# One step more between a tile's mask and its norm in an attention pipeline, with one guard and one reciprocal for two tiles

## The chip, the cores and the metric

The kernel runs on one core of one Trainium2 chip. The metric is the device time of one execution in microseconds (us). The kernel before takes 1290.63 us, the median of three runs that lie between 1290.49 and 1290.71 us.

The engines are named as in the profile: PE is TensorE's matrix multiply and PEld its weight load, DVE is VectorE, ACT is ScalarE, POOL is GpSimd, SP is SyncE. L309 is line 309 of the kernel file.

## The reference

Three stages follow one another. Attention has 2 batches, 8 heads, 576 rows and head dimension 64; its softmax keeps only scores within `tau` of the row's largest. Then a mixture of 8 experts with a gate that is normalised eight times over rows and columns, and a mixture of 4 experts with given probabilities, both on 1152 rows of 512 columns with 1024 hidden columns.

```python
def _attn_ref(q, k, v, tau):
    scores = (1.0 / np.sqrt(q.shape[-1])) * np.matmul(q, k.transpose(0, 1, 3, 2))
    thresh = np.max(scores, axis=-1, keepdims=True) - tau
    scores = np.where(scores >= thresh, scores, -1000000000.0)
    scores = scores - np.max(scores, axis=-1, keepdims=True)
    attn = np.exp(scores)
    attn = attn / (np.sum(attn, axis=-1, keepdims=True) + 1e-09)
    return np.matmul(attn, v).astype(np.float32)

def _moe_ref(x, w_gate, w1, w2):          # x: 1152 x 512
    P = np.exp(x @ w_gate - (x @ w_gate).max())
    for _ in range(8):
        P /= P.sum(1, keepdims=True) + 1e-09
        P /= P.sum(0, keepdims=True) + 1e-09
        P *= N / E
    for e in range(8):
        out += P[:, e:e + 1] * (np.maximum(x @ w1[e], 0.0) @ w2[e])

def _moe2_ref(x, domain_probs, w1, w2):
    p = domain_probs / (domain_probs.sum(-1, keepdims=True) + 1e-09)
    for e in range(4):
        out += p[:, e:e + 1] * (np.maximum(x @ w1[e], 0.0) @ w2[e])
```

The row sum in the denominator, the 1e-9 that is added to it and the division are what the change touches.

## The kernel before

**Units.** Attention is cut into 72 units (tiles) of 128 rows of queries against all 576 keys. The first 16 units (`exact` in the code) are rows 0 to 255 of batch 0; the next 20 the other 320 rows of batch 0, five for each pair of heads; the last 36 are batch 1, nine for each pair. Products that need more than one pass are made from a rounded high part and a low part (`kh` and `kl`, `eth` and `etl`); the 16 exact units transpose and multiply in fp32 instead, without a low part.

**Steps.** `step` (L415 to L462) is called once for each step t and issues, in program order, one piece of work for each of several units; the order on every engine is this order. In step t before:

- PE transposes unit t-2 into `et` and `er` (`turn`, L327 and L329), and later in the step makes the scores of unit t+2 (L275 for the first four units, L282 after), and the product with v for a unit that ended a group (`mix`, L367 for exact units, L374 and L376 for the others).
- DVE masks unit t (L309: score at or above the threshold times the exponential, in place, with the row sum as a second output), takes the row maximum of unit t+1 (`top`, L287), adds 1e-9 to the sum of unit t (`guard`, L313), works out the threshold of unit t+1 where the unit is exact (`line`, L295 to L298), and takes the reciprocal for unit t (L317). Further down the step it makes the low part of unit t-2's transposed tile (`lo`, L349 and L352) and adds or splits outputs (L385, L396, L502).
- POOL scales unit t in place by the reciprocal (`norm`, L319). It also splits keys, values and weights (L85, L109) and prepares queries (L253 to L257).
- ACT casts unit t-2's transposed tile to its high part (`hi`, L334 and L336), takes the exponential of unit t+1 (L303 or L305), and, for units that aren't exact, its threshold (L292).

There are 72 + 5 steps and a start of two.

**Buffers.** Four exponential tiles `ex` go round, six statistics tiles `st`, one transposed tile `et` (so the next `turn` waits for `hi` and `lo` of the unit before), and two score tiles in use at a time.

**Work beside attention.** `plan` (L194) sets the step in which keys, queries and values of a head are prepared. From unit 16 on, two fillers of an expert layer are issued between the scores and the next transposes (`expert_fill`: L493 and L521 on PE, L499 and L525 on ACT, L502 on DVE); the list `todo` (L592) says from which step each may start, `few` (L598) how many pieces a step may take near the batch border. The rest of the expert layers runs when attention has ended.

Of the kernel before, what the change touches and what calls it, by code (L numbers as in the profile page):

```python
# [9 lines left out]
F32 = mybir.dt.float32  # L10
F32R = mybir.dt.float32r
AF = mybir.ActivationFunctionType
ALU = mybir.AluOpType
# [6 lines left out]
P = 128  # L20
# [5 lines left out]
RA1, RA2 = 3, 4  # L26
# [3 lines left out]
def attention_two_moe_kernel(ctx, tc, qP, kP, qT, kT, vp, tau, wg, w1, w1s, w2, w2s, dp, m2w1s, m2w2, m2w2s, out):  # L30
    nc = tc.nc
    V, A, G, T = nc.vector, nc.scalar, nc.gpsimd, nc.tensor
# [9 lines left out]
    acc = [accp.tile([P, DM], F32, name=f"acc{t}") for t in range(4)]  # L42
# [79 lines left out]
    class Attention:  # L122
# [71 lines left out]
        def plan(self):  # L194

            for i, hd in enumerate(self.heads):
                if hd["ws"]:
                    continue
                old = self.heads[i - 2]
                k, q = i - 4, i - 3  # L200
                v = hd["first"] + 3
                if not old["ws"]:
                    k, v = max(hd["first"] - 5, old["end"] - 2), max(v, old["lastmix"] + 3)
                    q = k + 1
                    if hd["n"] == S and hd["h"] % 2 == 0:
                        v = max(hd["first"] + 2, old["lastmix"] + 3)
                for t, w in zip((k, q, v), self.prep(hd)):
                    self.work.setdefault(t, []).append(w)

# [73 lines left out]
                             start=i == 0, stop=i == len(ops) - 1)  # L283

        def top(self, u):
            st = u["st"] = self.pl.tile([P, 8], F32, tag="st", name="st", bufs=6)
            V.tensor_reduce(st[:, 0:1], u["sc"][:, :, :HS], axis=AX.XY, op=ALU.max, negate=not u["q"][0][0]["ws"])  # L287

        def line(self, u):
# [17 lines left out]
        def mask(self, u):  # L307
            st, ex = u["st"], u["ex"]
            V.scalar_tensor_tensor(ex, u["sc"][:, :, :HS], st[:, 2:3], ex, op0=ALU.is_ge, op1=ALU.mult,  # L309
                                   accum_out=st[:, 3:4])  # L310

        def guard(self, u):
            V.tensor_scalar(u["st"][:, 4:5], u["st"][:, 3:4], 1e-9, None, op0=ALU.add)  # L313

        def norm(self, u):
            st = u["st"]
            V.reciprocal(st[:, 5:6], st[:, 4:5])  # L317
            exf = u["exf"] = u["ex"].rearrange("p a b -> p (a b)")
            G.tensor_scalar(exf, exf, st[:, 5:6], 1.0, op0=ALU.mult, op1=ALU.mult)  # L319

        def turn(self, u):
            eg, exf = u["eg"], u["exf"]
# [92 lines left out]
        def step(self, fill, side):  # L415

            us, t = self.units, self.t
            un = lambda i: us[i] if 0 <= i < len(us) else None
            self.load()
            nxt, a, d, x, c, z, y = (un(t + i) for i in (2, 1, 0, -2, -3, -4, -5))  # L420
            if x:
                self.turn(x)
            if d:
                self.mask(d)
            if a:
                self.top(a)
            if d:
                self.guard(d)
            if a and a["q"][0][0]["exact"]:
                self.line(a)  # L430
            if d:
                self.norm(d)
            for part, u in ((2, y), (1, z), (0, c)):
                for g in u["mix"] if u else ():
                    if g["head"]["exact"]:
                        self.mix(g, part)
            if x:
                self.hi(x)
            for u, late in ((z, False), (y, True)):
                for g in u["mix"] if u else ():  # L440
                    if late == g["head"]["exact"]:
                        self.out(g)
            if a:
                self.exp(a)
                if not a["q"][0][0]["exact"]:
                    self.line(a)
            fill(0, bool(c and c["mix"]))
            if x:
                self.lo(x)
            if nxt:  # L450
                self.scores(nxt)
            self.run(self.later)
            for g in c["mix"] if c else ():
                if not g["head"]["exact"]:
                    self.mix(g, 0)
            fill(1, bool(c and c["mix"] or z and z["mix"]))
            self.run(self.late)
            for w in self.work.pop(t, ()):
                w()
            side()  # L460
            self.t += 1
            return self.t < len(us) + 5  # L462


    def start(t):
# [71 lines left out]
    y1 = [early[:, DM * t:DM * (t + 1)] for t in range(4)]  # L537

    def part(t, at, k, n):
        return t[:, at:at + k * n].rearrange("p (k n) -> p k n", k=k)  # L540

    tail0 = [[part(tails, 512 * j, FT, 64) for j in range(2)],
             [part(tails, 1024 + 1024 * j, FT, P) for j in range(2)]]
# [4 lines left out]
    with ExitStack() as att:  # L548
        ap = pool(att, "attn", side="right")
        ps_s = pool(att, "ps_s", 2, space=PSUM)  # L550
        ps_t = pool(att, "ps_t", 1, space=PSUM)
        ps_r = pool(att, "ps_r", 1, space=PSUM)
        banks.pool = ps = pool(att, "ps_m", 2, space=PSUM)
        at = Attention(ap, ps_s, ps_t, ps_r, ps)
        for p in range(H // 2):
            at.add_pair(0, p, 0, 256, True, p == 0)
        nA0 = len(at.units)
        for p in range(H // 2):
            at.add_pair(0, p, 256, 320, False)
        nA1 = len(at.units)  # L560
        for p in range(H // 2):
            at.add_pair(1, p, 0, S, False)
        at.plan()
        room = [2 * FT]
        at.load()
        drop = on[:, 0:1]
        V.tensor_scalar(drop, tau_sb, 0.0, None, op0=ALU.is_ge)
        V.tensor_scalar(esc, drop, 0.125, None, op0=ALU.mult)
        V.tensor_scalar(lin[:, 0:1], drop, -0.125, None, op0=ALU.mult)
        V.tensor_scalar(drop, drop, -BIG, BIG, op0=ALU.mult, op1=ALU.add)  # L570
        V.scalar_tensor_tensor(lin[:, 1:2], tau_sb, 8.0, drop, op0=ALU.mult, op1=ALU.add)
        V.tensor_tensor(drop, tau_sb, drop, op=ALU.add)
        V.tensor_scalar(on[:, 1:2], drop, -1.0, None, op0=ALU.mult)

        def side():
            if at.t >= -1:
                fetch(2)
            if at.t >= nA0 - 3 and raws and room[0] and (at.t % 3 < 2 if at.t < nA1 else room[0] > 2 or at.t % 2):
                room[0] -= 1
                cook()  # L580
            if at.t == 20:
                nc.sync.dma_start(wg_sb, wg)
                nc.sync.dma_start(dp_sb, dp)
            if at.t == 24:
                split(V, V, wg2[:, :, :E1], wg2[:, :, E1:], wg_sb)

        def free(n):
            room[0] += n

        X0, X1 = Expert(0), Expert(1)  # L590
        near, far = ((0, 0), (1, P)), ((2, 32), (3, 32 + P))
        todo = [(nA0 + 4, expert_fill(hp, X0, 0, 256, near, acc, None, 0, at.later, keep)),  # L592
                (nA1 + 3, expert_fill(hp, X0, 256, 320, far, acc, tail0[0], 0, at.later, free)),
                (nA1 + 3, expert_fill(hp, X1, 0, 256, near, y1, None, 0, at.later, keep)),
                (nA1 + 3, expert_fill(hp, X1, 256, 320, far, y1, tail0[1], 0, at.later, keep))]

        left, spent = [0], [0]
        few = dict(zip(range(nA1 - 3, nA1 + 4), (2, 2, 2, 2, 2, 1, 1)))  # L598

        def pull(n, end=True):  # L600

            for i in range(n):
                if not todo or at.t <= todo[0][0] or (left[0] == 1 and not end):
                    return i
                left[0] = next(todo[0][1], -1)
                if left[0] < 0:
                    todo.pop(0)
                if left[0] <= 0:
                    left[0] = 0
                    return i + 1  # L610
            return n

        def fill(phase, busy):
            if phase == 0:
                if 0 <= at.t < nA0 - 3 and at.t % 2 == 0:
                    room[0] -= 1
                    cook()
                spent[0] = pull(few.get(at.t, 3))
            elif left[0] or not busy:
                pull(max(few.get(at.t, RA1 if at.t < nA1 + 3 else RA2) - spent[0], 0), True)  # L620

        while at.step(fill, side):
            pass
        at.flush()
        while left[0]:
            pull(1)
        at.flush()
        while raws:
            cook()
            fetch(2)  # L630
# [25 lines left out]
    class Psum:  # L656
# [17 lines left out]
        def pair(self):  # L674
            whole = [(self.free.index(k), k ^ 1) for k in self.free if k ^ 1 in self.free[:self.free.index(k)]]
            if not whole:
                return None
            k = self.free[min(whole)[0]] & ~1
            return self.take(k, k + 1)
# [861 lines left out]
```

## Time and profile before

| | us |
|---|---|
| median of three runs | 1290.63 |
| the profiled execution's own time | 1290.54 |
| its span in the trace | 1288.8 |
| attention (first scores to the last product with v) | about 6 to 243 |
| PE busy in the whole span | 1268.6 |
| DVE busy in the whole span | 877.0 |

The profiled execution's own time stands 1.74 us above its span and 0.09 us under the median of the runs. Attention fills about the first fifth of the span; what comes behind it is the rest of the expert layers. Busy times that the trace gives for PE are of a pipelined engine, so a stretch can be called fully busy while matmuls still start late; the list of waits says what ended the idle times.

### The profile page before, as it was taken

What the parts mean: (1) busy time and instruction counts of PE and PEld (TensorE: products, weight loads), DVE (VectorE), ACT (ScalarE), POOL (GpSimd) and SP (SyncE); (2) the same over time, 40 slices, a digit from 0 to 9 for tenths busy, and PEclk for the clock granted to TensorE, in tenths of its full rate; (3) what the DMA queues carried; (4) which work ended last, traced back from release to release, by engine and by line L of the source; (5) the groups of instructions that cost most, each with busy time, mean ns of one, the idle gap of its engine ahead of it and who ended that gap; (6) DMA issues with size and microseconds to landing.
All of it is one profiled execution on the core that took longest, in us unless ns stands there. A gap on an engine that the chain in (4) does not pass through costs nothing.

```text
span 1288.8 us, 25100 instructions
## 1 busy us (share of the span) xinstructions
PE 1268.6 (98%) x9373; PEld 1207.6 (94%) x9373; DVE 877.0 (68%) x1842; ACT 739.1 (57%) x1492; POOL 896.9 (70%) x987
## 2 busy tenths in 40 slices
PE   8998999999999999999999999999999999999998
PEld 5597988888889999999999999999989999999998
DVE  6798888567537666766666666676745667666667
ACT  7887877422546646555554655566546465555552
POOL 7997987405796776867777786777668568677760
PEclk9999999999999999999999999999999999999999
DMA  5542330101221111212111211111212012111102
GB/s 171 160 128 75 97 97 17 41 1 34 66 83 50 42 42 50 58 35 58 50 42 42 52 59 37 52 50 42 58 34 59 25 50 58 35 57 50 42 18 74
DMA packets 43225, 73.84 MB, mean 57 GB/s; under 512 B 5216, under 2 KB 12512, under 8 KB 43104
## 3 DMA queue, kind: packets, MB, share of 16 engines
q1 hardware_dynamic: 42816, 71.96, 19.3%
q8 instruction: 74, 1.21, 0.4%
q14 instruction: 47, 0.39, 0.1%
q10 hardware_dynamic: 288, 0.28, 0.1%
HBM read 69.86 MB, written 2.36 MB: 56 GB/s over the span
## 4 chain that ended last, share of the span: by engine, by line
PE 89%; DVE 4%; POOL 2%; ACT 2%; issue 1%; DMA 1%; SPq 0%; DVEq 0%; POOLq 0%; ACTq 0%
PE mm L1079 36%; PE mm L1391 33%; PE mm L493 5%; PE mm L521 5%; PE mm L1199 3%; PE sc L282 2%; PE et L327 2%; PE pv L367 1%; DVE ex L309 1%; PE pv L376 1%; PE pv L374 1%; DVE st L287 1%; DVE etl L349 1%; ACT ex L305 0%; POOL wl L85 0%
## 5 line engine op out<-in xcount | busy, mean ns | idle before, releaser
L85 POOL TENSOR_TENSOR wl<-raw,wh 128x512 fp32r<-128x512 f32 x217 | 282.3, 1307 | 181.1 <-ACT wh L80 180.9
L1179 DVE SCALAR_TENSOR_TENSOR acc<-mm,p,acc 128x256 f32<-128x256 f32 (+1 forms) x428 | 195.3, 508 | 72.2 <-PE mm L1391 59.3
L1391 PE MATMUL mm<-wh,h 128*128 128x256 f32 x960 | 173.6, 279 | 0.0
L1086 ACT COPY snap<-mm 128x576 f32<-128x576 f32 x126 | 80.9, 642 | 152.5 <-DVE mm L1240 77.9
L80 ACT CAST wh<-raw 128x512 fp32r<-128x512 f32 x217 | 133.5, 627 | 47.2 <-PE mm L1391 26.4
L1391 PEld LDWEIGHTS mm<-wh,h 128*128 128x128 f32 x960 | 146.6, 188 | 0.0
L1079 PE MATMUL mm<-xh,wl 128*128 128x288 f32 x672 | 145.6, 297 | 0.3
L1079 PE MATMUL mm<-xh,wh 128*128 128x288 f32 x672 | 143.4, 294 | 0.0
L1079 PE MATMUL mm<-xl,wh 128*128 128x288 f32 x672 | 143.0, 294 | 0.0
L1391 PE MATMUL mm<-wl,h 128*128 128x256 f32 x480 | 134.6, 280 | 0.0
L1391 PE MATMUL mm<-wh,tails 128*128 128x256 f32 x696 | 126.4, 279 | 0.0
L85 POOL TENSOR_TENSOR wl<-sum,wh 128x512 fp32r<-128x512 f32 x82 | 107.4, 1310 | 8.1 <-ACT wh L80 8.1
L1079 PEld LDWEIGHTS mm<-xh,wl 128*128 128x128 f32 x672 | 106.3, 188 | 3.3 <-DVE mm L1099 0.5
L1079 PE MATMUL mm<-xth,wl 128*128 128x288 f32 x504 | 108.2, 295 | 0.2
L1079 PE MATMUL mm<-xtl,wh 128*128 128x288 f32 x504 | 107.8, 294 | 0.0
L1079 PE MATMUL mm<-xth,wh 128*128 128x288 f32 x504 | 107.5, 294 | 0.0
L1079 PEld LDWEIGHTS mm<-xl,wh 128*128 128x128 f32 x672 | 107.4, 188 | 0.0
L1079 PEld LDWEIGHTS mm<-xh,wh 128*128 128x128 f32 x672 | 107.2, 188 | 0.0
L1391 PEld LDWEIGHTS mm<-wh,tails 128*128 128x128 f32 x696 | 106.2, 188 | 0.0
L80 ACT CAST wh<-sum 128x512 fp32r<-128x512 f32 x82 | 51.5, 628 | 85.4 <-POOL sum L783 72.0
L1391 PE MATMUL mm<-wl,tails 128*128 128x256 f32 x348 | 97.3, 279 | 0.0
L1391 PEld LDWEIGHTS mm<-wl,h 128*128 128x128 f32 x480 | 90.0, 188 | 0.4
(241 smaller groups left out, 3486.2 us busy)
## 6 DMA issues: line engine op xcount, KB each, us to landing
raw<-in_w1s SPq DMA_DIRECT2D x56, 256.0 KB, 2.7
raw<-in_w2s SPq DMA_DIRECT2D x48, 256.0 KB, 2.6
raw<-in_w SPq DMA_DIRECT2D x40, 256.0 KB, 3.1
raw<-in_m2w1s SPq DMA_DIRECT2D x32, 256.0 KB, 2.6
raw<-in_m2w2s SPq DMA_DIRECT2D x28, 256.0 KB, 2.6
kr<-in_kT SPq DMA_DIRECT2D x22, 288.0 KB, 3.1
vr<-in_vp SPq DMA_DIRECT2D x24, 160.0 KB, 2.6
qr<-in_qT SPq DMA_DIRECT2D x8, 288.0 KB, 2.9
```

Of the source, the lines that this page charges most:

```text
L80: A.copy(hi, src)
L85: el.tensor_tensor(lo, src, f(hi), op=ALU.subtract)
L282: T.matmul(sc[:m, hf, :HS], lhsT=q, rhs=kk[:, hf * HS:(hf + 1) * HS], start=i == 0, stop=i == len(ops) - 1)
L287: V.tensor_reduce(st[:, 0:1], u["sc"][:, :, :HS], axis=AX.XY, op=ALU.max, negate=not u["q"][0][0]["ws"])
L327: T.transpose(et[:, kt], exf[:, kt * P:(kt + 1) * P], ident)
L493: T.matmul(ph[:, :n], lhsT=a[:, kt * P:(kt + 1) * P], rhs=x[:, kt, n0:n0 + n], start=i == 0 and kt == 0, stop=i == 2 and kt == KT - 1)
L521: T.matmul(py, lhsT=x, rhs=a, start=i == 0, stop=i == 3 * FT - 1)
L1079: T.matmul(ch[b][:, g, :HS], lhsT=w[:, (2 * g + kt) * P:(2 * g + kt + 1) * P], rhs=operand(u, kt, lo), start=first and j == 0, stop=j == l ...
L1086: A.copy(v[u], m)
L1179: V.scalar_tensor_tensor(a, src, s, a, op0=ALU.mult, op1=ALU.add)
L1199: T.matmul(py, lhsT=hid[x][:, kk, o:o + P], rhs=w[y], start=n == 0, stop=n == 3 * HF - 1)
L1391: T.matmul(m, lhsT=hid(x, kt + ko), rhs=wk[y], start=first and n == 0, stop=n == 5, skip_group_check=True)
```

## The change

The step loop gets one stage more. `mask` puts the row sum of unit t into a tile `two` of eight columns that two units share (an even and the odd unit behind it): columns 0 and 1 hold the two sums, 2 and 3 the sums with 1e-9, 4 and 5 the reciprocals. `guard` runs in odd steps alone, behind `top`, and makes both additions and both reciprocals with two instructions of 128x2. `norm` on POOL scales unit t-1 instead of unit t. `turn` is unit t-3 instead of t-2, the products with v and the outputs come one step later too, and the steps end at 72 + 6. The plan for values, the starts in `todo` and the numbers in `few` are one step later; the preparation of keys and queries stays where it was. `st` has three buffers instead of six, `two` has three.

```diff
--- before.py
+++ after.py
@@ -198,12 +198,12 @@
                     continue
                 old = self.heads[i - 2]
                 k, q = i - 4, i - 3
-                v = hd["first"] + 3
+                v = hd["first"] + 4
                 if not old["ws"]:
-                    k, v = max(hd["first"] - 5, old["end"] - 2), max(v, old["lastmix"] + 3)
+                    k, v = max(hd["first"] - 5, old["end"] - 2), max(v, old["lastmix"] + 4)
                     q = k + 1
                     if hd["n"] == S and hd["h"] % 2 == 0:
-                        v = max(hd["first"] + 2, old["lastmix"] + 3)
+                        v = max(hd["first"] + 3, old["lastmix"] + 4)
                 for t, w in zip((k, q, v), self.prep(hd)):
                     self.work.setdefault(t, []).append(w)
 
@@ -283,7 +283,7 @@
                              start=i == 0, stop=i == len(ops) - 1)
 
         def top(self, u):
-            st = u["st"] = self.pl.tile([P, 8], F32, tag="st", name="st", bufs=6)
+            st = u["st"] = self.pl.tile([P, 8], F32, tag="st", name="st", bufs=3)
             V.tensor_reduce(st[:, 0:1], u["sc"][:, :, :HS], axis=AX.XY, op=ALU.max, negate=not u["q"][0][0]["ws"])
 
         def line(self, u):
@@ -307,16 +307,21 @@
         def mask(self, u):
             st, ex = u["st"], u["ex"]
             V.scalar_tensor_tensor(ex, u["sc"][:, :, :HS], st[:, 2:3], ex, op0=ALU.is_ge, op1=ALU.mult,
-                                   accum_out=st[:, 3:4])
-
-        def guard(self, u):
-            V.tensor_scalar(u["st"][:, 4:5], u["st"][:, 3:4], 1e-9, None, op0=ALU.add)
+                                   accum_out=u["sum"])
+
+        def pair(self, i):
+            if i % 2 == 0:
+                self.two = self.pl.tile([P, 8], F32, tag="two", name="two", bufs=3)
+            u = self.units[i]
+            u["sum"], u["over"] = (self.two[:, k + i % 2:k + i % 2 + 1] for k in (0, 4))
+
+        def guard(self):
+            V.tensor_scalar(self.two[:, 2:4], self.two[:, 0:2], 1e-9, None, op0=ALU.add)
+            V.reciprocal(self.two[:, 4:6], self.two[:, 2:4])
 
         def norm(self, u):
-            st = u["st"]
-            V.reciprocal(st[:, 5:6], st[:, 4:5])
             exf = u["exf"] = u["ex"].rearrange("p a b -> p (a b)")
-            G.tensor_scalar(exf, exf, st[:, 5:6], 1.0, op0=ALU.mult, op1=ALU.mult)
+            G.tensor_scalar(exf, exf, u["over"], 1.0, op0=ALU.mult, op1=ALU.mult)
 
         def turn(self, u):
             eg, exf = u["eg"], u["exf"]
@@ -417,19 +422,20 @@
             us, t = self.units, self.t
             un = lambda i: us[i] if 0 <= i < len(us) else None
             self.load()
-            nxt, a, d, x, c, z, y = (un(t + i) for i in (2, 1, 0, -2, -3, -4, -5))
+            nxt, a, d, e, x, c, z, y = (un(t + i) for i in (2, 1, 0, -1, -3, -4, -5, -6))
             if x:
                 self.turn(x)
             if d:
+                self.pair(t)
                 self.mask(d)
             if a:
                 self.top(a)
-            if d:
-                self.guard(d)
+            if d and t % 2:
+                self.guard()
             if a and a["q"][0][0]["exact"]:
                 self.line(a)
-            if d:
-                self.norm(d)
+            if e:
+                self.norm(e)
             for part, u in ((2, y), (1, z), (0, c)):
                 for g in u["mix"] if u else ():
                     if g["head"]["exact"]:
@@ -459,7 +465,7 @@
                 w()
             side()
             self.t += 1
-            return self.t < len(us) + 5
+            return self.t < len(us) + 6
 
 
     def start(t):
@@ -589,13 +595,13 @@
 
         X0, X1 = Expert(0), Expert(1)
         near, far = ((0, 0), (1, P)), ((2, 32), (3, 32 + P))
-        todo = [(nA0 + 4, expert_fill(hp, X0, 0, 256, near, acc, None, 0, at.later, keep)),
-                (nA1 + 3, expert_fill(hp, X0, 256, 320, far, acc, tail0[0], 0, at.later, free)),
-                (nA1 + 3, expert_fill(hp, X1, 0, 256, near, y1, None, 0, at.later, keep)),
-                (nA1 + 3, expert_fill(hp, X1, 256, 320, far, y1, tail0[1], 0, at.later, keep))]
+        todo = [(nA0 + 5, expert_fill(hp, X0, 0, 256, near, acc, None, 0, at.later, keep)),
+                (nA1 + 4, expert_fill(hp, X0, 256, 320, far, acc, tail0[0], 0, at.later, free)),
+                (nA1 + 4, expert_fill(hp, X1, 0, 256, near, y1, None, 0, at.later, keep)),
+                (nA1 + 4, expert_fill(hp, X1, 256, 320, far, y1, tail0[1], 0, at.later, keep))]
 
         left, spent = [0], [0]
-        few = dict(zip(range(nA1 - 3, nA1 + 4), (2, 2, 2, 2, 2, 1, 1)))
+        few = dict(zip(range(nA1 - 2, nA1 + 5), (2, 2, 2, 2, 2, 1, 1)))
 
         def pull(n, end=True):
 
@@ -617,7 +623,7 @@
                     cook()
                 spent[0] = pull(few.get(at.t, 3))
             elif left[0] or not busy:
-                pull(max(few.get(at.t, RA1 if at.t < nA1 + 3 else RA2) - spent[0], 0), True)
+                pull(max(few.get(at.t, RA1 if at.t < nA1 + 4 else RA2) - spent[0], 0), True)
 
         while at.step(fill, side):
             pass
```

On DVE, among the exact units (`xl` is the low part of an output): what a step holds before the change.

```order
L309 SCALAR_TENSOR_TENSOR ex,st<-sc,st,ex 128x576
L287 TENSOR_REDUCE st<-sc 128x1
L313 TENSOR_SCALAR st<-st 128x1
L295 TENSOR_SCALAR st<-st,on 128x1
L317 RECIPROCAL st<-st 128x1
L385 TENSOR_TENSOR xl<-pv,xh 64x256
```

An even and an odd step of the same units on DVE after:

```order
L309 SCALAR_TENSOR_TENSOR ex,two<-sc,st,ex 128x576
L287 TENSOR_REDUCE st<-sc 128x1
L295 TENSOR_SCALAR st<-st,on 128x1
L309 SCALAR_TENSOR_TENSOR ex,two<-sc,st,ex 128x576
L287 TENSOR_REDUCE st<-sc 128x1
L319 TENSOR_SCALAR two<-two 128x2
L320 RECIPROCAL two<-two 128x2
L295 TENSOR_SCALAR st<-st,on 128x1
L390 TENSOR_TENSOR xl<-pv,xh 64x256
```

An even step has lost both small instructions; an odd step has them side by side, ahead of the threshold (L295) instead of around it.

On DVE, a step later in attention, where a low part `etl` is made in each step (L349 before, L354 after; `hl` is the low part of an expert's hidden tile). Before:

```order
L309 SCALAR_TENSOR_TENSOR ex,st<-sc,st,ex 128x576
L287 TENSOR_REDUCE st<-sc 128x1
L313 TENSOR_SCALAR st<-st 128x1
L317 RECIPROCAL st<-st 128x1
L349 TENSOR_TENSOR etl<-et,eth 128x4x128
L502 SCALAR_TENSOR_TENSOR hl<-mm,hh 128x256
```

After, from an even step's low part over an odd step to the next even one:

```order
L354 TENSOR_TENSOR etl<-et,eth 128x4x128
L357 TENSOR_TENSOR eth<-er,eth 64x384
L508 SCALAR_TENSOR_TENSOR hl<-mm,hh 128x256
L309 SCALAR_TENSOR_TENSOR ex,two<-sc,st,ex 128x576
L287 TENSOR_REDUCE st<-sc 128x1
L319 TENSOR_SCALAR two<-two 128x2
L320 RECIPROCAL two<-two 128x2
L354 TENSOR_TENSOR etl<-et,eth 128x4x128
L508 SCALAR_TENSOR_TENSOR hl<-mm,hh 128x256
L309 SCALAR_TENSOR_TENSOR ex,two<-sc,st,ex 128x576
L287 TENSOR_REDUCE st<-sc 128x1
L354 TENSOR_TENSOR etl<-et,eth 128x4x128
```

In odd steps the low part still stands behind both small instructions, in even steps it follows the maximum directly. In all DVE has 36 guards and 36 reciprocals instead of 72 and 72.

On PE, the start of the program, with the tiles' numbers (`sc` are score tiles, `ex` the unit that is transposed). Before:

```order
L275 MATMUL sc_222<-y1_97 128x288 x2
L327 MATMUL et_225<-ident_68,ex_163 128x128 x4
L329 MATMUL er_226<-ident_68,ex_163 64x128
L282 MATMUL sc_247<-kh_155,qs_168 128x288 x2
L282 MATMUL sc_247<-kl_156,qs_168 128x288 x2
L327 MATMUL et_254<-ident_68,ex_192 128x128 x4
L329 MATMUL er_226<-ident_68,ex_192 64x128
```

After:

```order
L275 MATMUL sc_220<-y1_97 128x288 x2
L282 MATMUL sc_236<-kh_155,qs_168 128x288 x2
L282 MATMUL sc_236<-kl_156,qs_168 128x288 x2
L332 MATMUL et_243<-ident_68,ex_163 128x128 x4
L334 MATMUL er_244<-ident_68,ex_163 64x128
L282 MATMUL sc_260<-kh_155,qs_168 128x288 x2
L282 MATMUL sc_260<-kl_156,qs_168 128x288 x2
```

The scores of the fifth unit now stand ahead of the first transposes, and so on down the program: every transposition and product with v stands one unit's scores later. PE's number of instructions is the same.

## Rows read from the trace of the kernel before

**Rows 1.** The page: busy us of the span, and the chain by engine.

```profile
PE 1268.6 (98%) x9373; PEld 1207.6 (94%) x9373; DVE 877.0 (68%) x1842; ACT 739.1 (57%) x1492; POOL 896.9 (70%) x987
...
PE 89%; DVE 4%; POOL 2%; ACT 2%; issue 1%; DMA 1%; SPq 0%; DVEq 0%; POOLq 0%; ACTq 0%
```

**Rows 2.** Busy us of each engine in stretches of 50 us, with instruction counts.

```profile
0.00:50.00 50.00, 44.04 (x199) 27.30 (x200) 33.88 (x117) 39.80 (x77) 39.09 (x48) 1.00 0.57 167
50.00:100.00 50.00, 47.84 (x324) 39.94 (x325) 43.62 (x113) 41.45 (x94) 46.49 (x57) 1.00 0.45 131
100.00:150.00 50.00, 47.17 (x322) 43.72 (x321) 44.72 (x114) 40.07 (x88) 39.85 (x63) 1.00 0.28 79
...
250.00:300.00 50.00, 50.00 (x311) 43.54 (x310) 33.49 (x94) 13.70 (x35) 15.09 (x14) 1.00 0.04 12
```

**Rows 3.** PE waits from 20 to 250 us: total us, times, longest.

```profile
PE et L327 <- DVE etl L349: 3.9, 7, 1.6
PE sc L282 <- DVE ex L309: 2.2, 4, 1.0
...
PE mm L493 <- DVE xf L396: 0.7, 1, 0.7
```

**Rows 4.** Timeline of DVE: start, us, instruction, idle before and releaser.

```profile
179.92 0.69 DVE L349 TENSOR_TENSOR etl<-et,eth 128x512 fp32r<-128x512 f32 x1 [1.80 <-ACT eth L334]
```

**Rows 5.** Chain of waits at the start: start us, us, what.

```profile
13.95 1.06 PE et L327 x4
...
15.03 0.59 ACT e L334
15.62 0.74 ACT ex L303
...
23.07 0.63 PE et L327 x4
23.70 0.11 PE er L329
23.80 1.72 PE pv L367 x6
25.53 0.73 PE sc L282 x4
...
26.80 1.01 PE pv L367 x4
...
29.09 1.72 PE pv L367 x6
```

**Rows 6.** All L313: ns min, median, max; who waited for it.

```profile
L313 DVE TENSOR_SCALAR st<-st x72: 136/144/154, 9.4 to 231.6; 128x1 f32<-128x1 f32 x72
...
  ACT ex L305: 15.0, 21
```

**Rows 7.** All L317: ns min, median, max; who waited for it.

```profile
L317 DVE RECIPROCAL st<-st x72: 152/164/167, 9.8 to 231.8; 128x1 f32<-128x1 f32 x72
...
  POOL ex L319: 8.8, 9
```

**Rows 8.** Timeline of DVE in one step near 116 us.

```profile
115.28 0.75 DVE L287 TENSOR_REDUCE st<-sc 128x1 f32<-128x576 f32 x1
115.95 0.14 DVE L313 TENSOR_SCALAR st<-st 128x1 f32<-128x1 f32 x1
116.13 0.17 DVE L317 RECIPROCAL st<-st 128x1 f32<-128x1 f32 x1
116.21 0.67 DVE L349 TENSOR_TENSOR etl<-et,eth 128x512 fp32r<-128x512 f32 x1
```

**Rows 9.** Chain of waits from 195 to 206 us.

```profile
198.40 0.73 DVE ex L309 x2
...
199.89 0.74 ACT ex L305
...
204.82 1.29 PE mm L493 x9
```
## The prediction

> **What bounds the kernel now.** I read the page's busy line and chain first, then busy time by stretch, then what ends PE's waits in attention, and last the places where the removed instructions stand. PE is busy for 1268.6 of 1288.8 us and the chain that ends last lies 89% on PE and 4% on DVE [rows 1]. The change edits attention alone, and by the stretches that is also where PE isn't full: 44.04 of the first 50 us, 47.84 and 47.17 of the next two, then 50.00 of 50 as soon as attention is over [rows 2]. So what attention ends earlier or later goes to the end one for one: behind it PE never waits, and its instructions are the same in number and order.
>
> Where PE waits in attention for DVE, the list of waits from 20 to 250 us has three large entries: 3.9 us in 7 waits of a transposition for the low part of the unit before, 2.2 us in 4 of scores for a mask, 0.7 us in one of an expert piece for an output [rows 3]. That is 6.8 us in 12 waits. The longest, 1.6 us, isn't DVE's: its low part at 179.92 us came after 1.80 us in which DVE itself waited for ACT's cast [rows 4]. There remain 5.2 us in 11 waits.
>
> **The change part by part.**
>
> *The small instructions.* 72 guards and 72 reciprocals before, medians 144 and 164 ns [rows 6, 7], become 36 and 36 on two columns. In one step DVE starts the guard at 115.95 and the next large instruction at 116.21 [rows 8]: the two cost 0.26 us of DVE's time, less than their durations add up to, since each begins before the one ahead has ended. So 36 steps save 0.26 us each, 9.4 us in all. That two columns cost more than one isn't shown here; bounds are the same 0.26 us and, if each column paid anew, 0.52 us (then nothing is saved). I take the same, because the row of one column is nearest: a maximum over 576 columns takes some 0.67 us from start to start, a guard over one 0.18 [rows 8], so columns are cheap and the start is dear.
>
> [...]
>
> Of the 9.4 us only what stands ahead of something that PE waits for counts. The two instructions stand between the maximum and the low part in every step [rows 8], so in the even steps the low part, and with it the next transposition, is 0.26 us earlier; in the odd steps it is where it was. Of 11 waits about half fall into even steps: 5.5 x 0.26 = 1.4 us. Beyond that, where the chain stays with DVE for several steps, as from 198.40 to PE's release at 204.82 but for one exponential at 199.89 [rows 9], time saved in one step is handed to the next; for that I take two more of 0.26, 0.5 us. Sum: 1.9 us gained. Bounds: nothing (each wait is ended by something else a moment later), and all of the 5.2 us.
>
> The 15.0 us that ACT's exponential waited for a guard and the 8.8 us that POOL's norm waited for a reciprocal [rows 6, 7] look like more, but they aren't. An exponential needs the maximum, which ends just ahead of the guard; the guard is only the last thing that DVE did. It starts as early after the change. POOL's wait goes for the odd units (their reciprocal stands a step ahead) and stays for the even ones; the norm's result is wanted by a transposition two steps later, before and after.
>
> *The extra step.* Each transposition and product with v is one step later against the scores. At the end the expert fillers cover it: as many of their products stand ahead of the last product with v as before. At the start nothing does. Once PE is the bound (from 23.07 us) an exact step takes 2.65 us, half of the 5.29 us between two like groups of products at 23.80 and 29.09 [rows 5]. Of that, scores (0.73) are done early, and the transposition (0.44 to 0.63 + 0.11) and half of the products (1.72 + 1.01, so 1.37) late. So at the same scores PE has about 0.55 + 1.44 = 2.0 us more left (five products of 1.72/6 us). Against it, PE comes to those scores earlier: the first transpositions (1.06 us at 13.95, slow there) no longer stand ahead of the fifth scores, and ACT's cast of 0.59 us at 15.03 no longer ahead of an exponential at 15.62 [rows 5]. That is worth 0.59 and some part of 1.06; I take 1.0 in all. Net: 1.0 us lost. Bounds: 0 (the start hides all of it) and a whole step, 2.65 us.
>
> *The moves.* Values are split a step later and the fillers start a step later, both against scores and with their users; the query casts on ACT and the query work on POOL now stand one step earlier against the casts of transposed tiles. PE waits for such casts too (the 1.6 us above). It can fall either way: I take 0 and, as bounds, 1.6 us less and 1.6 us more. `st` with three buffers is used for two steps, so no wait comes of it. An exponential now also follows the transposition of the unit four before it in the same step (the four `ex` tiles live a step longer), but ACT's cast of that same transposition stands ahead of it on ACT anyway: 0.
>
> **The sum.** 1290.54 (the profiled execution) + 1.0 - 1.9 + 0 = 1289.6 us. The median of the runs stands 0.09 us above that execution, so 1289.7 us.
>
> **Rivals.**
>
> (a) *DVE paces attention, and its saving carries over.* For it: DVE is busy 43 to 45 of 50 us from 50 to 150 us, so its pauses are few, and most of PE's waits end with DVE [rows 2, 3]; a step's late start is then the next step's too. Against it: PE is busy 47 of 50 there. Then all of the 5.2 us go: 1290.6 + 1.0 - 5.2 = 1286.4 us. [...]
>
> (b) *The other side: the start costs its whole step and DVE's saving is hidden.* Place: the exact units, where from 23.07 us on PE runs without a break and the two small instructions aren't on the chain at all [rows 5]. Price 2.65 us; if the later waits are ended by ACT or POOL instead of DVE, nothing comes back: 1290.6 + 2.65 = 1293.3 us. It decides from the point where the gain at DVE is under 0.05 us. For it: the gain is only in every other step, and the odd steps keep both instructions. Against it: PE has idle time at the start (5.96 us of the first 50 [rows 2]) that an earlier fifth score can fill.
>
> (c) *Nothing comes of it.* Gains and the extra step cancel, or PE's order hides both: 1290.6 us.
>
> **How the numbers follow.** Chances: my forecast 0.45, (a) 0.27, (b) 0.13, (c) 0.15. The time is the forecast's, 1289.7 us. About 0.2%, 2.6 us, is what a measurement of this kernel can tell from no change: faster is below 1288.0, slower above 1293.2. Faster gets nearly all of (a) and a seventh of the forecast: 0.31. Slower gets most of (b) and a little of the forecast, where the moves fall badly: 0.12. Same: 0.57. The range reaches down to 1286.0, just past (a), and up to 1292.8, most of the way to (b); beyond it lies a tenth on either side. The forecast's own range is 1287.9 to 1291.6.
>
> **What would show it.** In the profile of the changed kernel: 36 guards and 36 reciprocals of about 0.15 us; the low part directly behind the maximum in even steps; waits of transpositions for the low part down from 3.9 us to some 2 to 3; the chain at the start with exact steps still of 2.65 us, and attention's end (the last product with v) about 1 us earlier than at 243 us; behind it PE full as before. If the waits for low parts go away altogether, (a) was right; if attention ends at 245 or later, (b). What would make it wrong otherwise is a new long wait of PE for POOL or ACT in attention, where the moved query work meets the casts, of the size of the 1.6 us, several times over.

## The result, and the profile after

The changed kernel takes 1297.85 us (median of six runs, 1297.65 to 1299.33) against 1290.67 us before (six runs, 1290.49 to 1291.05): 1.0058 times, interval 1.0048 to 1.0067. It is 7.2 us slower; 1289.7 us was forecast, with a range up to 1292.8. The span of the profiled execution went from 1288.8 to 1295.9 us.

The page after, engines' busy times and the chain by engine:

```profile
PE 1271.2 (98%) x9373; PEld 1208.7 (93%) x9373; DVE 884.5 (68%) x1770; ACT 739.5 (57%) x1492; POOL 898.1 (69%) x987
...
PE 86%; DVE 6%; ACT 4%; POOL 3%; issue 1%; DMA 0%; SPq 0%; DVEq 0%; ACTq 0%; POOLq 0%
```

DVE has 72 instructions fewer than in [rows 1] and is busy for 7.5 us longer. That is the line to stop at: fewer instructions, more time. Grouped by line, DVE's two small instructions after (count, then busy us and mean ns):

```profile
L319 DVE TENSOR_SCALAR two<-two 128x2 f32<-128x2 f32 x36 | 18.0, 501 | 0.0
L320 DVE RECIPROCAL two<-two 128x2 f32<-128x2 f32 x36 | 6.0, 166 | 1.2
```

The reciprocal on two columns takes 166 ns, as one column did [rows 7]. The guard on two columns takes 501 ns on average, where one column took 144 [rows 6]. All of its 36 in one line (min, median, max):

```profile
L319 DVE TENSOR_SCALAR two<-two x36: 158/425/2121, 12.1 to 235.0; 128x2 f32<-128x2 f32 x36
```

So its own work is some 158 ns, and the rest, 18.0 - 36 x 0.158 = 12.3 us, comes and goes. What it goes with is seen when DVE's and POOL's timelines are laid side by side. DVE, in a step near 143 us (start, length, instruction):

```profile
142.50 0.76 DVE L287 TENSOR_REDUCE st<-sc 128x1 f32<-128x576 f32 x1
143.16 1.42 DVE L319 TENSOR_SCALAR two<-two 128x2 f32<-128x2 f32 x1
144.62 0.17 DVE L320 RECIPROCAL two<-two 128x2 f32<-128x2 f32 x1
144.70 0.67 DVE L354 TENSOR_TENSOR etl<-et,eth 128x512 fp32r<-128x512 f32 x1
```

POOL in the same stretch:

```profile
143.13 1.43 POOL L85 TENSOR_TENSOR kl<-kr,kh 128x576 fp32r<-128x576 f32 x1
144.96 0.75 POOL L324 TENSOR_SCALAR ex<-ex,two 128x576 f32<-128x576 f32 x1 [0.40 <-DVE two L320]
```

POOL begins its 1.43 us at 143.13 and ends at 144.56; the guard begins 0.03 us later and ends at 144.58. The profile shows no wait between them: POOL splits keys there and the guard adds 1e-9 to two numbers. Of the 36 guards 27 take more than 0.2 us, and each of these 27 ends within 0.03 us behind the end of an instruction on POOL. The longest, 2.12 us at 158.81, stands still through two instructions of POOL one behind the other. And PE, for which the low part behind the guard is made:

```profile
145.51 0.63 PE L332 MATMUL et<-ident,ex 128*128 128x128 f32 x4 [0.98 <-DVE etl L354]
```

A guard on one column does not stand still like that. In the kernel before, the guard of [rows 8] ran its 0.14 us at 115.95, inside the same kind of split on POOL:

```profile
114.74 1.44 POOL L85 TENSOR_TENSOR kl<-kr,kh 128x576 fp32r<-128x576 f32 x1 [0.30 <-ACT kh L80]
```

Of the 72 guards before, 57 began and ended inside an instruction on POOL, and none took more than 0.154 us [rows 6]. POOL is seldom idle in attention: [rows 2] has it busy for 46.49 us of the 50 from 50 to 100, a column that the prediction didn't weigh.

The list of PE's waits from 20 to 250 us, after (total us, times, longest), against [rows 3]:

```profile
PE et L332 <- DVE etl L354: 8.0, 12, 1.5
PE sc L282 <- DVE ex L309: 1.8, 4, 1.0
...
PE mm L499 <- DVE xf L401: 0.7, 1, 0.7
```

Waits for the low part have doubled, from 3.9 to 8.0 us. By stretches, in the columns of [rows 2]:

```profile
0.00:50.00 50.00, 42.90 (x192) 26.80 (x193) 35.67 (x101) 38.55 (x75) 38.82 (x47) 1.00 0.57 169
50.00:100.00 50.00, 47.92 (x323) 39.70 (x322) 43.20 (x96) 41.79 (x95) 46.40 (x58) 1.00 0.47 135
100.00:150.00 50.00, 45.90 (x307) 41.76 (x306) 44.66 (x96) 38.85 (x85) 37.45 (x57) 1.00 0.25 68
...
250.00:300.00 50.00, 48.95 (x302) 42.13 (x301) 30.14 (x84) 13.18 (x35) 12.62 (x23) 1.00 0.09 30
```

PE is 1.3 us less busy from 100 to 150 us, and one wait of about 1 us that stood just ahead of 250 us before now falls behind it. The last product with v tells where attention ends (first and last start stand behind the times in ns); before:

```profile
L376 PE MATMUL pv<-eth,vhl x120: 277/307/313, 67.8 to 242.7; 128*128 128x320 f32 x80, 128*128 128x256 f32 x40
```

and after:

```profile
L381 PE MATMUL pv<-eth,vhl x120: 276/307/315, 70.5 to 248.2; 128*128 128x320 f32 x80, 128*128 128x256 f32 x40
```

Attention ends 5.5 us later. The first of these products is 2.7 us later, which is the extra step. The remaining 1.6 us come behind attention, in five places some 90 us apart. They show as "issue" (no releaser in the trace) in the group of L1185, where an expert's output is added up on DVE; before, the group is L1179, with the same two main releasers and no "issue":

```profile
L1185 DVE SCALAR_TENSOR_TENSOR acc<-mm,p,acc 128x256 f32<-128x256 f32 (+1 forms) x428 | 196.2, 508 | 74.1 <-PE mm L1397 59.4 <-PE mm L1205 9.6 <-issue 1.2
```

Five times 0.23 us in which DVE waits for nothing that the trace shows; against the kernel before, PE is 0.31 us further behind after each. The pauses stand 128 DVE instructions apart, and 0.9 us behind the start of each an 8192-byte packet of the queue q14, of kind `instruction`, begins. But the span holds 46 packets of that queue and kind, and the pauses are five, so what causes them was not shown.

### The profile page after: what moved, and what is told of

It reads as the page before. It is cut to its first block, busy times and chain, and to the rows that moved or that the text cites. A ratio compares the mean times of both kernels' runs of the same rounds, so it can differ in the third digit from the quotient of the medians.

```text
span 1295.9 us, 24982 instructions
## 1 busy us (share of the span) xinstructions
PE 1271.2 (98%) x9373; PEld 1208.7 (93%) x9373; DVE 884.5 (68%) x1770; ACT 739.5 (57%) x1492; POOL 898.1 (69%) x987
## 4 chain that ended last, share of the span: by engine, by line
PE 86%; DVE 6%; ACT 4%; POOL 3%; issue 1%; DMA 0%; SPq 0%; DVEq 0%; ACTq 0%; POOLq 0%
PE mm L1085 36%; PE mm L1397 32%; PE mm L527 5%; PE mm L499 3%; PE mm L1205 3%; PE sc L282 2%; PE pv L372 2%; PE et L332 2%; DVE ex L309 1%; POOL wl L85 1%; DVE st L287 1%; ACT ex L305 1%; DVE etl L354 1%; PE pv L381 1%; DVE two L319 1%
## 5 line engine op out<-in xcount | busy, mean ns | idle before, releaser
L1185 DVE SCALAR_TENSOR_TENSOR acc<-mm,p,acc 128x256 f32<-128x256 f32 (+1 forms) x428 | 196.2, 508 | 74.1 <-PE mm L1397 59.4
```

Source lines behind the costliest of these rows:

```text
L1185: V.scalar_tensor_tensor(a, src, s, a, op0=ALU.mult, op1=ALU.add)
```

## The experiments

Two theories were put against one another. Theory 1: the guard on two columns waits for the instruction that POOL runs, and that is the loss. Theory 2: the extra step and what it moves are the loss. Later runs ask what makes the guard wait: two columns, neighbouring columns, or two inputs. Each ratio is to runs of the kernel before that were taken beside it (medians 1290.14 to 1290.67 us), so ratios compare better than times.

| run | us | ratio to before, interval | guard, sum us | waits for low part, us | last product with v, us |
|---|---|---|---|---|---|
| the change | 1297.85 | 1.0058, 1.0048 to 1.0067 | 18.0 in 36 | 8.0 | 248.2 |
| two guards of one column | 1290.04 | 0.9998, 0.9989 to 1.0007 | 10.3 in 72 | 2.8 | 242.3 |
| before, guard of two columns | 1302.51 | 1.0092, 1.0079 to 1.0106 | 37.4 in 72 | 12.0 | 254.5 |
| longer pipeline alone | 1290.53 | 1.0002, 0.9993 to 1.0011 | 10.3 in 72 | 2.7 | 242.7 |
| change without guard | 1288.87 | 0.9990, 0.9981 to 0.9999 | none | 2.3 | 241.5 |
| sums four columns apart | 1297.96 | 1.0057, 1.0043 to 1.0070 | 18.0 in 36 | 8.0 | 248.2 |
| guard with two inputs | 1296.27 | 1.0046, 1.0034 to 1.0059 | 17.7 in 36 | 8.0 | 248.1 |
| before without guard | 1289.61 | 0.9992, 0.9983 to 1.0001 | none | 3.6 | 241.4 |
| one memset more | 1296.23 | 1.0046, 1.0032 to 1.0060 | 18.3 in 36 | 7.8 | 247.9 |
| guard on ACT | 1300.07 | 1.0075, 1.0062 to 1.0088 | 10.2 in 36, on ACT | 2.0 | 250.5 |

### Two guards of one column

```diff
-            V.tensor_scalar(self.two[:, 2:4], self.two[:, 0:2], 1e-9, None, op0=ALU.add)
+            for k in range(2):
+                V.tensor_scalar(self.two[:, 2 + k:3 + k], self.two[:, k:k + 1], 1e-9, None, op0=ALU.add)
```

> The changed kernel with its guard of 128x2 written as two guards of 128x1 behind one another; all else as changed. [...] Theory 2 (the extra step and the moved casts and query work cost the 7 us): 1297.5 to 1299, since one instruction more in odd steps saves nothing.

Measured: 1290.04 us. One instruction more in every odd step, and 7.8 us less. The guards of this kernel:

```profile
L320 DVE TENSOR_SCALAR two<-two x72: 133/143/153, 12.0 to 229.1; 128x1 f32<-128x1 f32 x72
```

None takes more than 153 ns, although 55 of the 72 begin and end inside a running POOL instruction. Theory 2 is out.

### The kernel before, with a guard of two columns

```diff
-            V.tensor_scalar(u["st"][:, 4:5], u["st"][:, 3:4], 1e-9, None, op0=ALU.add)
+            V.tensor_scalar(u["st"][:, 4:6], u["st"][:, 2:4], 1e-9, None, op0=ALU.add)
...
-            V.reciprocal(st[:, 5:6], st[:, 4:5])
+            V.reciprocal(st[:, 6:7], st[:, 5:6])
```

(POOL's norm reads column 6 instead of 5.)

> The kernel before, its pipeline untouched, with one edit: each of the 72 guards is 128x2 instead of 128x1 (the second column is the threshold plus 1e-9 and isn't used), the reciprocal stays on one column. Theory 1: the guards wait for POOL here too, 0.3 us each on average, 20 to 27 us in all on DVE, and as in the changed kernel more than half of it comes through to the end: 1300 to 1308 us. Theory 2: one column more costs nothing: 1290.7 us (1290.3 to 1291.3).

Measured: 1302.51 us. With no change to the pipeline, one column more on the guard costs 12 us:

```profile
L313 DVE TENSOR_SCALAR st<-st x72: 151/384/3207, 9.4 to 243.2; 128x2 f32<-128x2 f32 x72
```

Here 48 of the 72 take more than 0.2 us, and all 48 end with an instruction on POOL. The dose fits: 37.4 - 72 x 0.151 = 26.5 us of waiting moved attention's end by 11.8 us, 45% of it. In the changed kernel 12.3 us moved it by 5.9 against the same kernel with two guards of one column (248.2 and 242.3), 48%. No run took work away from POOL; that POOL is what the guard waits for rests on these ends that coincide and on the guards of one column that run beside POOL.

### The longer pipeline alone

```diff
-            V.tensor_scalar(self.two[:, 2:4], self.two[:, 0:2], 1e-9, None, op0=ALU.add)
-            V.reciprocal(self.two[:, 4:6], self.two[:, 2:4])
+            k = self.t % 2
+            V.tensor_scalar(self.two[:, 2 + k:3 + k], self.two[:, k:k + 1], 1e-9, None, op0=ALU.add)
+            V.reciprocal(self.two[:, 4 + k:5 + k], self.two[:, 2 + k:3 + k])
...
-            if d and t % 2:
+            if d:
                 self.guard()
```

> The changed kernel's longer pipeline (norm, transpositions, products with v one step later) with a guard of 128x1 and a reciprocal of 128x1 for every unit in every step, so 72 and 72 as before. Theory 1: the extra step alone costs 0 to 2.7 us: 1291.6 us (1290.3 to 1293.3). Theory 2: 1297 to 1299 us, the changed kernel's time or a little above, with the waits of transpositions for the low part still at about 8 us.

Measured: 1290.53 us, no difference from before. Its products with v:

```profile
L382 PE MATMUL pv<-eth,vhl x120: 277/307/315, 70.4 to 242.7; 128*128 128x320 f32 x80, 128*128 128x256 f32 x40
```

The first is 2.6 us later than before and the last at the same 242.7 us. The extra step is paid at the start, as forecast, and given back by the end of attention.

### The change without the guard

```diff
-            V.tensor_scalar(self.two[:, 2:4], self.two[:, 0:2], 1e-9, None, op0=ALU.add)
-            V.reciprocal(self.two[:, 4:6], self.two[:, 2:4])
+            V.reciprocal(self.two[:, 4:6], self.two[:, 0:2])
```

> The changed kernel with the guard left out (the addition of 1e-9 is left out of the computation); the reciprocal of 128x2 takes the sums themselves. In the changed kernel the reciprocal on two columns takes 166 ns and shows no wait. Theory 1: DVE has 0.26 us less in even steps and some 0.2 less in odd ones, no wait for POOL: 1290.6 + 1.0 - 2.4, about 1289.2 us (1286.5 to 1291.5). Theory 2: 36 guards of 0.5 us gone are worth a few us by their length alone, but the extra step's 7 us stay: 1294 to 1297.5.

Measured: 1288.87 us, the fastest of all, 0.1% under before. The reciprocal on two columns waits for nobody:

```profile
L319 DVE RECIPROCAL two<-two 128x2 f32<-128x2 f32 x36 | 5.6, 155 | 0.0
```

Each row's largest score gives an exponential of one, so the sum is at least one and 1e-9 is too small to change it in fp32; who accepts that has here a version that is 9 us under the change. Its gain of 1.3 us on the kernel before is small, and the interval of its ratio ends just under one (0.9999).

### The sums four columns apart

```diff
-            u["sum"], u["over"] = (self.two[:, k + i % 2:k + i % 2 + 1] for k in (0, 4))
+            u["sum"], u["over"] = (self.two[:, k + i % 2 * 4:k + i % 2 * 4 + 1] for k in (0, 2))
...
-            V.tensor_scalar(self.two[:, 2:4], self.two[:, 0:2], 1e-9, None, op0=ALU.add)
-            V.reciprocal(self.two[:, 4:6], self.two[:, 2:4])
+            V.tensor_scalar(self.two[:, 1:8:4], self.two[:, 0:8:4], 1e-9, None, op0=ALU.add)
+            V.reciprocal(self.two[:, 2:8:4], self.two[:, 1:8:4])
```

> The changed kernel with the two sums four columns apart (columns 0 and 4, the guard's outputs 1 and 5, the reciprocals 2 and 6), so that the guard's 128x2 isn't two neighbouring words. Theory 1a (two elements in a row of a one-source instruction are enough, whatever their distance): guards of 0.15 to 2.1 us again, 18 us in all, time 1297 to 1299. Theory 1b (only neighbouring words are taken as a pair): guards of 0.15 us, 5.5 us in all, time about 1290, as with two guards of one column less 36 instructions (1289 to 1290.5).

Measured: 1297.96 us.

```profile
L319 DVE TENSOR_SCALAR two<-two x36: 158/426/2123, 12.1 to 235.0; 128x2 f32<-128x2 f32 x36
```

Four columns apart or side by side makes no difference; that there are two elements does (1a).

### The guard with two inputs

```diff
+            self.tiny = pl.tile([P, 2], F32, name="tiny")
+            V.memset(self.tiny, 1e-9)
...
-            V.tensor_scalar(self.two[:, 2:4], self.two[:, 0:2], 1e-9, None, op0=ALU.add)
+            V.tensor_tensor(self.two[:, 2:4], self.two[:, 0:2], self.tiny, op=ALU.add)
```

> The changed kernel with the guard as an addition of two tiles in SBUF (the sums and a constant tile of 1e-9, 128x2 each) in place of the addition of a number. Theory 1c (an instruction with two inputs in SBUF waits for POOL just as one that reads one input twice as wide): guards of 0.4 us and more at the median, 1297 to 1299 us. Theory 1d (only the wide form of a one-source instruction waits): guards of about 0.15 us, 36 of them, DVE has 0.26 us less in even steps and some 0.1 more than that nowhere: 1289.0 to 1290.2 us, at or under both kernels.

Measured: 1296.27 us.

```profile
L321 DVE TENSOR_TENSOR two<-two,tiny x36: 149/418/2143, 12.1 to 234.9; 128x2 f32<-128x2 f32 x36
```

An addition of two tiles in SBUF waits just as long (1c), 27 of 36 again. The five pauses behind attention are gone, and the time lies 0.7 us under the range of 1c; the run with one memset more takes that up. Whether two inputs of one column wait wasn't run.

### The kernel before without the guard

```diff
         def guard(self, u):
-            V.tensor_scalar(u["st"][:, 4:5], u["st"][:, 3:4], 1e-9, None, op0=ALU.add)
+            V.reciprocal(u["st"][:, 5:6], u["st"][:, 3:4])
...
-            V.reciprocal(st[:, 5:6], st[:, 4:5])
```

> The kernel before with the guard left out (the addition of 1e-9 is left out of the computation) and the reciprocal of each unit in its place, ahead of the threshold; the pipeline is as before. It asks what the longer pipeline and the shared reciprocal are worth once no guard stands in the way (the changed kernel without guard took 1288.87 us). If the sharing is worth its 36 reciprocals: about 1289.8 us, between that and the 1290.1 of before. If leaving the guard out was all of that gain: 1288.5 to 1289.2 us.

Measured: 1289.61 us, 0.9992 (0.9983 to 1.0001) of before; the change without guard had 0.9990 (0.9981 to 0.9999). The two can't be told apart: what the longer pipeline and the 36 shared reciprocals add to a missing guard lies under 1 us, and this run doesn't say which of its two expectations holds.

### One memset more

```diff
+            self.tiny = pl.tile([P, 2], F32, name="tiny")
+            V.memset(self.tiny, 1e-9)
```

> The changed kernel with one unused instruction more on DVE, a memset of 128x2 ahead of attention. The changed kernel ends 1.6 us later behind attention than all others measured: at five places some 90 us apart DVE pauses for 0.23 us ahead of L1185 with nothing that the trace shows it waiting for, and PE loses 0.31 us each time; so does the kernel with the sums apart, which has the same number of DVE instructions, and not the one with two sources, which has one more. If the pauses hang on where an instruction stands in DVE's stream: they go, and the time is 1296.2 to 1296.5. If they come from how late attention ends or from the guard: 1297.6 to 1298.2, with the five pauses.

Measured: 1296.23 us, 1.6 us under the change, with a guard that waits as before (median 434 ns, 425 in the change). The same group as L1185 above, in this kernel:

```profile
L1187 DVE SCALAR_TENSOR_TENSOR acc<-mm,p,acc 128x256 f32<-128x256 f32 (+1 forms) x428 | 195.3, 508 | 72.4 <-PE mm L1399 59.5 <-PE mm L1207 9.5
```

"issue" is gone. One unused instruction in front shifts every later one in DVE's stream by one place, and the five pauses vanish. From the last product with v to the end the profiled executions take 1045.8 us before, 1047.4 in the change, 1046.3 here and 1046.0 with two inputs, so 1.1 to 1.4 of the 1.6 us come back with the pauses. They hang on where an instruction stands, not on the guard: the next kernel, whose guard isn't on DVE at all, has three such pauses of 0.23 us, at 1077, 1167 and 1258 us, again 128 DVE instructions apart. What happens at those places wasn't tried.

### The guard on ACT

```diff
-            V.tensor_scalar(self.two[:, 2:4], self.two[:, 0:2], 1e-9, None, op0=ALU.add)
+            A.activation(self.two[:, 2:4], self.two[:, 0:2], AF.Identity, bias=self.tiny[:, 0:1], scale=1.0)
...
-            if d and t % 2:
-                self.guard()
...
-            if e:
-                self.norm(e)
...
+            if d and t % 2:
+                self.guard()
             fill(0, bool(c and c["mix"]))
             if x:
                 self.lo(x)
+            if d and t % 2:
+                self.invert()
+            if e:
+                self.norm(e)
```

(`invert` is the reciprocal; `tiny` as above.)

> The changed kernel with the guard of two columns on ACT (an addition of a constant column of 1e-9) behind the exponential in odd steps, the reciprocal of two columns on DVE behind the low part, and POOL's norm behind that; nothing is left out. If the wait for POOL is DVE's alone, ACT's guard takes 0.2 to 0.3 us without a wait, DVE loses the guard from the way to the low part, and the time is 1288.8 to 1290.5. If ACT waits for POOL too, or the later norms hold up POOL's preparation of queries and so PE: 1291 to 1295.

Measured: 1300.07 us, above both expected ranges. ACT doesn't wait for POOL (285 ns on average), but DVE now waits for ACT in front of the reciprocal, and POOL for the late reciprocal:

```profile
L321 ACT ACTIVATE two<-two,tiny 128x2 f32<-128x2 f32 x36 | 10.2, 285 | 0.1
...
L324 DVE RECIPROCAL two<-two 128x2 f32<-128x2 f32 x36 | 6.0, 166 | 24.6 <-ACT two L321 24.4
...
L328 POOL TENSOR_SCALAR ex<-ex,two 128x576 f32<-128x576 f32 x72 | 53.6, 746 | 29.4 <-DVE two L324 26.3 <-ACT hh L511 1.9 <-PE et L336 0.4
```

DVE stands for 24.4 us in front of the reciprocal, with all its later work behind it, and 26.3 us of POOL's time stand in front of the norm, with the splits queued behind it. The waits for low parts are shorter than in any other run (2.0 us) and the kernel is the second slowest: the guard no longer waits, but DVE waits for ACT and POOL for DVE. Which of these waits carries the loss wasn't separated.

## Why the prediction was wrong

*What bounds the kernel:* right. PE bounds it, only attention changed in order, and what attention loses goes to the end one for one (5.5 us at its end, 5.5 us still there before the five pauses).

*The price of the guard on two columns:* here it failed. The step reads "bounds are the same 0.26 us and, if each column paid anew, 0.52 us (then nothing is saved). I take the same". It asked how long a second column takes and not what it makes the instruction do. Measured: 0.50 us for the guard alone instead of 0.144, up to 2.12, because it stands still while POOL runs. Both bounds were bounds on work, and the wait lies outside them: in place of 1.9 us gained, attention ends 5.5 us later than before (5.9 later than with two guards of one column). The working also says that each small instruction begins before the one ahead has ended; by [rows 8] that holds for the guard and the low part, but the reciprocal begins 0.04 us after the guard's end. The 0.26 us per pair stands all the same.

By shape, the runs showed this: the guard of 128x2 with one source waits (18.0 us in 36, side by side and four columns apart; 37.4 in 72 in the kernel before), and so does the one of 128x2 with two inputs (17.7 in 36). The guard of 128x1 doesn't (10.3 in 72, none above 0.155 us), and neither does the reciprocal on 128x2 (155 to 169 ns on average). Why these shapes and operations differ was not shown. One guard of the change, at 106.14 us, ran its 160 ns within a POOL instruction that had begun 0.08 us before, so not every overlap shows a wait.

*The saving on the way to the low part:* 1.9 us were forecast from 36 pairs less. No run has what the term describes, 36 guards that don't wait and 36 reciprocals. With two guards of one column, where DVE has 36 reciprocals less, nothing is measurable (0.9998, interval 0.9989 to 1.0007); without any guard 0.9990. By the ends of attention, 36 reciprocals less are worth 0.4 us (242.7 to 242.3) and the 72 guards 0.8 more (241.5). That makes some 0.8 us for 36 of each, an estimate from differences that the intervals don't clear. So the term was perhaps twice too large, which is small beside the 5.9.

*The extra step:* 1.0 us were forecast, of bounds 0 to 2.65. The first products with v are 2.6 us later, a whole step; at the end of attention nothing is left of it (242.7 us in both). The lower bound was right, and the reason given there ("the start hides all of it") wasn't: the start pays it, the rest of attention gives it back.

*The moves:* taken as 0. The longer pipeline alone holds them together with the extra step, and the two add up to nothing measurable (1.0002).

*The rivals:* (b) had the right side and the wrong cause: the time was slower because of an instruction that got longer, and neither the start nor hidden savings had a part in it. No rival named POOL as the one that DVE would wait for. The sign given for (b), attention ending at 245 us or later, came (248.2), yet its 1293.3 us is 4.6 us short as well. Of the forecast's own signs three failed: guards of about 0.15 us, waits for low parts down to 2 to 3 us, and an earlier end of attention. *What would make it wrong:* the last sentence looked for a long wait of PE for POOL in attention. It came, but by way of DVE, and the profile names DVE.

*Not foreseen at all:* 1.6 of the 7.2 us come with the five pauses behind attention, where the prediction had PE's end move one for one with attention's.

## What to carry to other kernels

That columns look cheap in [rows 8] doesn't make it free to fuse two one-column instructions into one of two columns: in these runs, next to a busy POOL, a guard of one column took at most 0.155 us and one of two columns up to 3.2. Before merging small DVE instructions, ask what POOL runs at that time, and whether the merged form goes from one column to two; here one column each was the form that never waited. Other widths weren't run. After such an edit look at min, median and max of the new instruction first: 158/425/2121 ns tells in one line that it waits and doesn't work.

## What the runs showed of the hardware that was not expected

- A `tensor_scalar` or `tensor_tensor` of 128x2 in fp32 within SBUF takes some 150 to 180 ns where it doesn't wait and up to 3.2 us next to a running POOL, ending within 0.03 us of the end of POOL's instruction in 27 of 27, 48 of 48, 27 of 27 and 27 of 27 cases that took more than 0.2 us. The trace books the wait as the instruction's own busy time, not as idle time, so neither the list of waits nor "idle before" names POOL.
- Somewhat under half of such waits on DVE came through to the end of attention: 48% of 12.3 us and 45% of 26.5 us.
- One unused instruction ahead removed five pauses of DVE of 0.23 us that lay between 458 and 819 us of the span, 128 DVE instructions apart; the time fell by 1.6 us.
